# w3's first two row blocks transposed by VectorE, the others by TensorE with every eighth column

## The chip, the cores and the metric

The kernel runs on one core of a Trainium2 chip. The metric is the time of one execution on the device, in microseconds, as the median of several runs. TensorE does the matrix products, VectorE (DVE), ScalarE (ACT) and GpSimd (POOL) the elementwise work, and SyncE (SP) issues the loads and stores. Each engine takes its instructions in the order in which the program wrote them for it, and waits for others through semaphores.

## The reference

Three parts follow one another. A decay attention over 32 heads of 576 tokens with 64 columns gives x of 2304 tokens by 512. A gated product follows, and then a rational function between two products:

```
x    = attention(q, k, v, f)                 # 2304 x 512
c    = (x @ w1) * (x @ w2)                   # 2304 x 1024
z    = (c @ w3) @ w_out                      # w3 1024 x 1024, w_out 1024 x 512
h    = z @ w_in                              # 2304 x 2048
out  = (P(h) / Q(h)) @ w_out2                # P cubic, Q with abs(h) and h*h
```

The weights arrive as 64-bit floats. The kernel reads them as pairs of 32-bit integers and works out 32-bit floats from them.

## The kernel before

Every large product is made of three passes: an operand is split into a high half that TensorE's fast format holds and a low half that is the rest, and high x high, high x low and low x high are added in one PSUM bank. The high half is a ScalarE copy, the low half a VectorE or GpSimd subtraction.

The kernel never forms c @ w3. It first folds w3 @ w_out into one weight of 1024 x 512 (`w3oh`, `w3ol`), and then takes z = c @ (w3 @ w_out). The stages that matter here follow one another on TensorE:

- The last a/b products (`gen_ab`, lines 709 to 738). For each of 8 column blocks of w1 and w2 and each half of the last batch's 576 tokens there are 12 instructions for a = x @ w1 and 12 for b = x @ w2, 288 columns each: 16 pairs. ScalarE copies a out of PSUM, VectorE multiplies it with b, and SP stores the result to `c_dr`. Those steps wait in the list `pend` and are written out by `flush(keep)`, which leaves `keep` of them. The last batch uses two pairs of banks: `ps_f` 0 and 1, and the two halves of `ps_v`.
- The w3 stage (lines 1114 to 1139). For each row block i of w3 (128 rows) the block is transposed, split, and multiplied with w_out: 8 column blocks j times 3 passes of 512 columns into `ps_f[i % 2]`, and the result is split into `w3oh[:, i]` and `w3ol[:, i]` (lines 1130 and 1131, the fold). Block i + 1 is transposed by TensorE ahead of column block 2 of row i: 8 transposes of 128 x 128 into `ps_s` or `ps_x`, and right behind them ScalarE's and VectorE's halves (lines 1072 and 1073). Block 0 is transposed ahead of everything.
- The z products (lines 1187 to 1211): 9 blocks of 256 tokens, 4 column blocks each, 24 instructions of 256 columns per column block.

The decoder `dec_` (class `Decoder`, lines 164 to 246) turns weights into floats beside all this. Its jobs are pieces of 128 rows by 256 columns: 4 of w3's block 0, 16 of w_out, then w3's blocks 1 to 7, then 32 of w_in. One call of `step()` works on four neighbouring jobs, one operation of each: the low half of job k - 3 (VectorE twice out of three, GpSimd once), the high half of k - 2 (ScalarE), the sum of k - 1 (GpSimd, line 227), the first two operations of job k (VectorE, lines 231 and 234) and its conversion (ScalarE, line 237), and then SP's load of a job ahead into a ring of four. For w3 the two halves are left out. `run(n)` takes steps until job n is finished.

The order of the work around the change is written by hand. While the last a/b products are written, the loop at line 1083 writes 1600 ns of products (at 123 ns each), flushes, and takes one decoder step: 28 steps in all. In the w3 stage four steps follow per row, after column blocks 3, 4, 5 and 7, and one in the last row; in the z products one step follows each column block. `w3r` holds six decoded row blocks of w3, so that blocks 6 and 7 come into the places of 0 and 1. `load_c` reads c back for the z products, and `split_c` splits it on ScalarE and VectorE, two column blocks each at the end of rows 3 to 6.

Of the kernel before, what the change touches and what calls it, by code (L numbers as in the profile page):

```python
# [15 lines left out]
ALU = mybir.AluOpType  # L16
# [3 lines left out]
P = 128  # L20
# [9 lines left out]
PIECE2 = 256  # L30
# [129 lines left out]
def raw(ap):  # L160
    return ap.bitcast(F32)


class Decoder:
# [22 lines left out]
    def prefetch(self):  # L187
        while self.sent < min(self.upcoming() + self.ahead, len(self.jobs)):
            r = self.ring[self.sent % len(self.ring)]
            src = self.jobs[self.sent][0]  # L190
            dst = r.rearrange("p n t -> p (n t)")
            if len(src.shape) == 3:
                dst = dst.rearrange("p (k n) -> p k n", k=src.shape[1])
            self.nc.sync.dma_start(dst, src.bitcast(I32))
            self.sent += 1
# [130 lines left out]
def kernel(  # L326
# [16 lines left out]
    nc = tc.nc  # L343
    B, H, S, D = q.shape
    NT, DM = out.shape
    DF1 = w1.shape[1]
# [3 lines left out]
    NF1 = DF1 // P  # L350
# [27 lines left out]
    ident = const.tile([P, P], F32, name="ident")  # L378
# [12 lines left out]
    ps_v = psp.tile([P, 1024], F32, name="ps_v")  # L391
    ps_s, ps_x = ([psp.tile([P, 512], F32, name=f"ps_{nm}{i}") for i in range(2)] for nm in "sx")
# [3 lines left out]
    ps_f = []  # L396
# [271 lines left out]

    w12 = {}

    def split(h, l):
        nc.scalar.copy(h, raw(l))  # L672
        nc.vector.tensor_tensor(out=l, in0=raw(l), in1=raw(h), op=ALU.subtract)  # L673

    def open_w12():
        wp = right1.enter_context(pool("w12", "right"))
# [32 lines left out]
    def gen_ab(b, more=()):  # L709
        banks = [*ps_f, *more]  # L710
        X, L = xh[b % 2], xl[b % 2]
        n = 0
        FG = PIECE2 // P
        for g, hf, fi in itertools.product(range(NF1 // FG), range(2), range(FG)):
            ts_ = slice(HB * hf, HB * (hf + 1))
            fi += FG * g
            fs = slice(P * fi, P * (fi + 1))
            w12["dec"].run(4 * g + 3)
            outs = [t[:, 0:HB] for t in banks[n % (len(banks) // 2) * 2 :][:2]]
            for wi, nm in enumerate(("w1", "w2")):  # L720
                wh, wl = w12[nm]
                flush(len(banks) // 2)
                for kc in range(NKC):
                    mm(outs[wi], wh[:, kc, fs], X[:, kc, ts_], kc == 0, False)
                    yield 123
                    mm(outs[wi], wh[:, kc, fs], L[:, kc, ts_], False, False)
                    yield 123
                    mm(outs[wi], wl[:, kc, fs], X[:, kc, ts_], False, kc == NKC - 1)
                    yield 123
                if wi == 0:  # L730
                    pend.append(lambda a=a_sb[n % 2], o=outs[0]: nc.scalar.copy(a, o))

            def finish(c=c_sb[n % 3], a=a_sb[n % 2], fi=fi, hf=hf, o=outs[1]):
                nc.vector.tensor_tensor(out=c, in0=o, in1=a, op=ALU.mult)
                nc.sync.dma_start(c_dr[:, fi, S * b + HB * hf : S * b + HB * (hf + 1)], c)

            pend.append(finish)
            n += 1

    fillers = []  # L740
# [3 lines left out]
    def flush(keep=0):  # L744
        while len(pend) > keep:
            pend.pop(0)()
# [81 lines left out]
    for t in range(NCH * (NH + 1) + 2):  # L828
        n, c = divmod(t, NCH)
        p, x = n // 2, t % 2  # L830
# [198 lines left out]
    d3.close()  # L1029
    late.close()  # L1030
    att.close()
    fillers.append(gen_ab(B - 1, (ps_v[:, 0:512], ps_v[:, 512:1024])))

    r2 = ExitStack()
    zp = r2.enter_context(pool("zp", "left"))
    w3oh = zp.tile([P, NF1, DM], F32R, name="w3oh")
    w3ol = zp.tile([P, NF1, DM], F32R, name="w3ol")
    w3p = ExitStack()
    jobs = []
    dec_ = Decoder(nc, zp, "d2", PIECE2, 4, 4, jobs, "vvg")  # L1040
# [4 lines left out]
    NR3 = 6  # L1045
# [4 lines left out]
    wq = w3q.enter_context(pool("w3q", "left"))  # L1050
    w3r += [wq.tile([P, DF1], F32, name=f"w3r{i}") for i in range(NF1 - NR3, NR3)]

    def w3_jobs(i):
        for g in range(0, DF1, PIECE2):
            cs = slice(g, g + PIECE2)
            jobs.append((w3[P * i : P * (i + 1), cs], w3r[i % NR3][:, cs], None, None))

    def w_jobs(w, j, h, l):
        for g in range(0, w.shape[1], PIECE2):
            cs = slice(g, g + PIECE2)  # L1060
            jobs.append((w[P * j : P * (j + 1), cs], None, h[:, j, cs], l[:, j, cs]))

    def w3_transpose(i, g):
        ps = (ps_s, ps_x)[i % 2][g]
        for j in range(4):
            k = 4 * g + j
            nc.tensor.transpose(
                ps[:, P * j : P * (j + 1)], w3r[i % NR3][:, P * k : P * (k + 1)], ident
            )
        src = ps.rearrange("p (j t) -> p j t", t=P)  # L1070
        h, l = (t[i % 2][:, 4 * g : 4 * g + 4] for t in (w3h, w3l))
        nc.scalar.copy(h, src)
        nc.vector.tensor_tensor(out=l, in0=src, in1=raw(h), op=ALU.subtract)

    w3_jobs(0)
    for j in range(NF1):
        w_jobs(w_out, j, woh, wol)
    for i in range(1, NR3):
        w3_jobs(i)
    dec_.prefetch()  # L1080
    credit[0] = 0.0
    fill(3000.0)
    while fillers:
        fill(1600.0)
        flush(2)
        dec_.step()
    flush()
    right1.close()

# [8 lines left out]
    def load_c(i):  # L1098
        for g in range(0, NF1, 2):
            nc.sync.dma_start(  # L1100
                raw(cl[i % 2][:, g : g + 2]), c_dr[:, g : g + 2, T1 * i : T1 * (i + 1)]
            )

    def split_c(i, g):
        split(ch[i % 2][:, g : g + 2], cl[i % 2][:, g : g + 2])

    for i in range(NR3, NF1):
        w3_jobs(i)
    at_w3 = {i: 4 * i + (3 if i == 0 else 19) for i in range(NF1)}
    for kc in range(NKC):  # L1110
        w_jobs(w_in, kc, wih, wil)
    dec_.prefetch()
    load_c(0)
    for i in range(NF1):
        if i == 0:
            w3_transpose(0, 0)
            w3_transpose(0, 1)
        po = ps_f[i % 2]
        for j in range(NF1):
            if j == 2 and i + 1 < NF1:  # L1120
                dec_.run(at_w3[i + 1])
                w3_transpose(i + 1, 0)
                w3_transpose(i + 1, 1)
            elif j in ((3, 4, 5, 7) if i + 1 < NF1 else (3,)):
                dec_.step()
            h, l = w3h[i % 2][:, j], w3l[i % 2][:, j]
            mm(po, h, woh[:, j], j == 0, False)
            mm(po, h, wol[:, j], False, False)
            mm(po, l, woh[:, j], False, j == NF1 - 1)
        nc.scalar.copy(w3oh[:, i], po)  # L1130
        nc.vector.tensor_tensor(out=w3ol[:, i], in0=po, in1=raw(w3oh[:, i]), op=ALU.subtract)  # L1131
        if i + 1 == NR3 - 1:
            w3q.close()
            cp1 = ctx.enter_context(pool("cp1", "right"))
            ch.append(cp1.tile([P, NF1, T1], F32R, name="ch1"))
            cl.append(cp1.tile([P, NF1, T1], F32R, name="cl1"))
            load_c(1)
        if 3 <= i < 7:
            split_c(0, 2 * (i - 3))
    w3p.close()  # L1140

    wl_ = ctx.enter_context(pool("wl", "right"))
# [218 lines left out]
```

## Time and profile before

| what | us |
|---|---|
| median of 3 runs (lowest and highest) | 987.3 (986.68 to 989.33) |
| the profiled execution, its own time | 988.95 |
| its span, first to last instruction | 987.1 |
| TensorE busy | 972.3 |
| VectorE busy | 765.3 |
| ScalarE busy | 658.6 |
| GpSimd busy | 391.3 |

The span begins with the first instruction and ends with the last; the profiled execution's own time also holds what lies around it. Busy times of engines overlap. TensorE's matrix instructions overlap one another, so that the start of the next one, not the length of a row, tells what one costs. The last a/b products end at about 426 us of the span, the w3 stage runs to 477.6 us, the z products to 580.7 us. Granted clock of TensorE: 0.998 in the mean.

### The profile page before, as it was taken

The page shows a single profiled execution, that of the slowest core. Times are in us where ns is not written, and L with a number is a line of the kernel's source. Part 1 is how long each engine was busy: PE and PEld are TensorE (multiplying, and loading weights), DVE is VectorE, ACT ScalarE, POOL GpSimd, SP SyncE. Part 2 cuts the span into 40 slices and gives each one's busy share as a digit, 9 for nine tenths or more (in the row PEclk, how much of TensorE's full clock was granted, in tenths as well). Part 3 has the DMA queues.
Part 4 walks back from the last instruction along what each step waited for, and adds up shares of the span by engine and source line. Part 5 has one row for each costly group of instructions (what it writes and reads, how often), then busy time and mean ns, then how long its engine had stood idle before and what let it go on. Part 6 is the DMA issues. An engine that isn't in the chain of part 4 may idle for free.

```text
span 987.1 us, 18112 instructions
## 1 busy us (share of the span) xinstructions
PE 972.3 (98%) x5964; PEld 855.8 (87%) x5964; DVE 765.3 (78%) x1753; ACT 658.6 (67%) x1435; POOL 391.3 (40%) x468
## 2 busy tenths in 40 slices
PE   8999999999999999999999999999999999999997
PEld 6777999999999999988899998888888888888886
DVE  5777887878888766979866439999787888877786
ACT  5777676767777653444555448887676767676686
POOL 7477666644554443534433103232222222222222
PEclk9999999999999999999999999999999999999999
DMA  5777665677777515565467570011001100100010
GB/s 153 168 196 189 171 145 125 170 194 196 186 185 189 164 65 171 197 197 192 156 219 223 173 239 31 1 43 43 1 0 43 43 1 22 43 0 1 1 43 23
DMA packets 146470, 113.62 MB, mean 115 GB/s; under 512 B 86660, under 2 KB 113292, under 8 KB 146376
## 3 DMA queue, kind: packets, MB, share of 16 engines
q1 hardware_dynamic: 146376, 112.46, 40.2%
q8 instruction: 47, 0.77, 0.3%
q14 instruction: 47, 0.39, 0.1%
HBM read 70.61 MB, written 23.22 MB: 95 GB/s over the span
## 4 chain that ended last, share of the span: by engine, by line
PE 88%; DVE 4%; ACT 3%; issue 2%; DMA 1%; POOL 1%; SPq 1%; POOLq 0%; ACTq 0%; DVEq 0%
PE bank L366 47%; PE ps_f L366 20%; PE ps_v L366 7%; PE ps_s L366 6%; PE ps_x L595 5%; PE ps_w L366 1%; PE ps_v L443 1%; ACT rr L1272 1%; ACT rr L1273 1%; DVE pr L564 1%; DMA d_r<-in_moe_w_in_dram 1%; DVE pp L1285 1%; ACT gh L1253 0%; DVE rr L1281 0%; DVE qv L1278 0%
## 5 line engine op out<-in xcount | busy, mean ns | idle before, releaser
L1254 POOL TENSOR_TENSOR gl<-pp,gh 128x512 fp32r<-128x512 f32 (+1 forms) x80 | 101.4, 1268 | 330.7 <-ACT gh L1253 318.8
L590 POOL TENSOR_SCALAR pr<-pr,st 128x128 f32<-128x128 f32 (+4 forms) x160 | 95.2, 604 | 118.9 <-DVE st L585 62.5
L366 PE MATMUL bank<-ch,wil 128*128 128x512 f32 (+1 forms) x320 | 118.2, 370 | 0.0
L366 PE MATMUL bank<-cl,wih 128*128 128x512 f32 (+1 forms) x320 | 118.1, 369 | 0.0
L564 DVE CUSTOM_DVE_ANT_0 pr<-ps_s,mask 128x128 f32<-128x128 f32 (+4 forms) x160 | 82.6, 521 | 45.7 <-PE ps_s L366 37.2
L366 PE MATMUL bank<-ch,wih 128*128 128x512 f32 (+1 forms) x320 | 117.8, 368 | 0.0
L366 PE MATMUL bank<-wo2h,gh 128*128 128x512 f32 x288 | 114.2, 397 | 0.8 <-ACT gh L1253 0.8
L366 PE MATMUL bank<-wo2h,gl 128*128 128x512 f32 x288 | 114.0, 396 | 0.3
L366 PE MATMUL bank<-wo2l,gh 128*128 128x512 f32 x288 | 113.9, 396 | 0.0
L575 ACT ACTIVATE pr<-pr,st 128x128 f32<-128x128 f32 (+4 forms) x160 | 97.2, 608 | 17.1 <-DVE st L564 10.7
L1261 ACT ACTIVATE h<-bank 128x512 f32<-128x512 f32 (+1 forms) x80 | 44.3, 554 | 81.2 <-PE bank L366 81.1
L1268 DVE SCALAR_TENSOR_TENSOR qv<-h,pb_abs,qv 128x512 f32<-128x512 f32 (+1 forms) x80 | 55.6, 695 | 36.6 <-ACT qv L1262 36.6
L366 PE MATMUL bank<-ch,w3ol 128*128 128x256 f32 x288 | 81.0, 281 | 0.5 <-DVE w3ol L1131 0.5
L366 PE MATMUL bank<-cl,w3oh 128*128 128x256 f32 x288 | 81.0, 281 | 0.3 <-DVE cl L673 0.3
L366 PE MATMUL bank<-ch,w3oh 128*128 128x256 f32 x288 | 80.9, 281 | 0.0
L595 PE MATMUL ps_x<-ident,pr 128*128 128x128 f32 (+1 forms) x480 | 74.9, 267 | 2.3 <-DVE ptl L621 0.7
L366 PE MATMUL ps_s<-kh,qs 128*128 128x128 f32 (+2 forms) x192 | 74.0, 388 | 2.7 <-DVE st L564 1.2
L1278 DVE SCALAR_TENSOR_TENSOR qv<-qv,rr 128x512 f32<-128x512 f32 (+1 forms) x80 | 51.4, 643 | 25.7 <-ACT rr L1273 25.7
L366 PEld LDWEIGHTS bank<-cl,wih 128*128 128x128 f32 x320 | 60.2, 188 | 11.7
L366 PEld LDWEIGHTS bank<-ch,wih 128*128 128x128 f32 x320 | 60.2, 188 | 11.7
L673 DVE TENSOR_TENSOR cl<-cl,ch 128x512 fp32r<-128x512 f32 (+1 forms) x56 | 39.5, 724 | 38.7 <-ACT ch L672 38.5
L366 PEld LDWEIGHTS bank<-ch,wil 128*128 128x128 f32 x320 | 60.2, 188 | 10.3
(180 smaller groups left out, 2991.1 us busy)
## 6 DMA issues: line engine op xcount, KB each, us to landing
d_r<-in_moe_w_dram SPq DMA_DIRECT2D x64, 256.0 KB
d_r<-in_moe_w_out_dram SPq DMA_DIRECT2D x48, 256.0 KB
c_dr<-c_sb SPq DMA_DIRECT2D x64, 144.0 KB
cl<-c_dr SPq DMA_DIRECT2D x36, 256.0 KB
d_r<-in_moe_w_in_dram SPq DMA_DIRECT2D x32, 256.0 KB
kh<-kh SPq DMA_DIRECT2D x42, 144.0 KB
z_dr<-z_sb SPq DMA_DIRECT2D x36, 128.0 KB
out_dram<-o_sb SPq DMA_DIRECT2D x18, 256.0 KB
```

The lines of the kernel that those rows point to most:

```text
L366: nc.tensor.matmul(o, lhsT, rhs, start=start, stop=stop)
L443: nc.tensor.transpose(ps[:, P * c : P * (c + 1)], flat(t[:, c]), ident)
L564: nc.vector.tensor_tensor_reduce(out=pr[0:r, OFF[c] + a : OFF[c] + b], in0=ps_s[(t + part) % 2][0:r, 0 : b - a], in1=mask[0:r, 512 - Q0[c] ...
L575: nc.scalar.activation(x, x, AF.Exp, bias=st[0:r, 0, c : c + 1], scale=-1.0, accum_out=se[0:r, c, 0:1],)
L590: nc.gpsimd.tensor_scalar(x, x, st[0:r, 1, c : c + 1], 1.0, op0=ALU.mult, op1=ALU.mult)
L595: nc.tensor.transpose(ps_x[x][:, r * j : r * (j + 1)], pr[0:r, o + P * j : o + P * (j + 1)], ident[0:r, 0:r],)
L673: nc.vector.tensor_tensor(out=l, in0=raw(l), in1=raw(h), op=ALU.subtract)
L1254: nc.gpsimd.tensor_tensor(out=at(gl, j), in0=at(pp, j), in1=raw(at(gh, j)), op=ALU.subtract)
L1261: nc.scalar.activation(at(h2, i), h, AF.Square)
L1268: nc.vector.scalar_tensor_tensor(out=at(qv, i), in0=at(h2, i), scalar=pb_abs[:, 1:2], in1=at(qv, i), op0=ALU.mult, op1=ALU.add,)
L1272: nc.scalar.activation(at(rr, i), at(qv, i), AF.Ln, bias=ln_bias, scale=2.0**-62)
L1278: nc.vector.scalar_tensor_tensor(out=at(qv, i), in0=at(qv, i), scalar=QC, in1=at(rr, i), op0=ALU.add, op1=ALU.mult)
```

## The change

- `gen_ab` for the last batch has three pairs of banks: `ps_x` 0 and 1 come to `ps_f` and the halves of `ps_v`. `flush` still leaves two entries.
- Blocks 0 and 1 of w3 are loaded in another form: one piece is 32 rows by all 1024 columns, where partition 32 a + r holds row r and columns 256 a to 256 a + 255. VectorE transposes each half (128 x 512) in blocks of 32 x 32 into PSUM, reading every eighth column, so that partition p then holds columns 8 p + k of w3 for k from 0 to 7.
- Blocks 2 to 7 are transposed by TensorE as before, but each transpose takes every eighth column (k, k + 8, ...) in place of 128 neighbouring ones. w_out's rows are loaded in the same order (row 8 p + k), so that the sum runs over the same terms.
- The split of a transposed block is now a step of its own (`w3_split`). Block 0 is transposed and split within the loop over the last a/b products, from decoder step 20 on, one part ahead of each step. For block i + 1 the two halves of the transpose are written ahead of column blocks 2 and 3 of row i, and the two splits ahead of column blocks 4 and 5.
- The fold of row i is written ahead of column block 2 of row i + 1. Decoder steps follow ahead of column blocks 0, 1, 6 and 7 of rows 0 to 4, ahead of column block 0 in rows 5 and 6, and not at all in row 7.
- All of w3's jobs are in the list from the beginning; w_in's follow after the loop.
- `split` and `split_c` get an argument for the engine of the subtraction, which every call leaves at VectorE.

```diff
--- before.py
+++ after.py
@@ -189,7 +189,9 @@
             r = self.ring[self.sent % len(self.ring)]
             src = self.jobs[self.sent][0]
             dst = r.rearrange("p n t -> p (n t)")
-            if len(src.shape) == 3:
+            if len(src.shape) == 3 and src.shape[0] < P:
+                pass
+            elif len(src.shape) == 3:
                 dst = dst.rearrange("p (k n) -> p k n", k=src.shape[1])
             self.nc.sync.dma_start(dst, src.bitcast(I32))
             self.sent += 1
@@ -668,9 +670,9 @@
 
     w12 = {}
 
-    def split(h, l):
+    def split(h, l, on=nc.vector):
         nc.scalar.copy(h, raw(l))
-        nc.vector.tensor_tensor(out=l, in0=raw(l), in1=raw(h), op=ALU.subtract)
+        on.tensor_tensor(out=l, in0=raw(l), in1=raw(h), op=ALU.subtract)
 
     def open_w12():
         wp = right1.enter_context(pool("w12", "right"))
@@ -719,7 +721,7 @@
             outs = [t[:, 0:HB] for t in banks[n % (len(banks) // 2) * 2 :][:2]]
             for wi, nm in enumerate(("w1", "w2")):
                 wh, wl = w12[nm]
-                flush(len(banks) // 2)
+                flush(min(len(banks) // 2, 2))
                 for kc in range(NKC):
                     mm(outs[wi], wh[:, kc, fs], X[:, kc, ts_], kc == 0, False)
                     yield 123
@@ -1029,7 +1031,7 @@
     d3.close()
     late.close()
     att.close()
-    fillers.append(gen_ab(B - 1, (ps_v[:, 0:512], ps_v[:, 512:1024])))
+    fillers.append(gen_ab(B - 1, (ps_v[:, 0:512], ps_v[:, 512:1024], *ps_x)))
 
     r2 = ExitStack()
     zp = r2.enter_context(pool("zp", "left"))
@@ -1050,40 +1052,73 @@
     wq = w3q.enter_context(pool("w3q", "left"))
     w3r += [wq.tile([P, DF1], F32, name=f"w3r{i}") for i in range(NF1 - NR3, NR3)]
 
+    NA, NB, ND = P // 32, DF1 // PIECE2, 2
+
     def w3_jobs(i):
-        for g in range(0, DF1, PIECE2):
-            cs = slice(g, g + PIECE2)
-            jobs.append((w3[P * i : P * (i + 1), cs], w3r[i % NR3][:, cs], None, None))
+        for g in range(NB):
+            r0 = P * i + 32 * g
+            if i < ND:
+                rows = w3[r0 : r0 + 32].rearrange("i (a n) -> a i n", a=NA)
+            else:
+                rows = w3[P * i : P * (i + 1), PIECE2 * g : PIECE2 * (g + 1)]
+            jobs.append((rows, w3r[i % NR3][:, PIECE2 * g : PIECE2 * (g + 1)], None, None))
 
     def w_jobs(w, j, h, l):
         for g in range(0, w.shape[1], PIECE2):
             cs = slice(g, g + PIECE2)
             jobs.append((w[P * j : P * (j + 1), cs], None, h[:, j, cs], l[:, j, cs]))
 
+    def w_out_jobs(j):
+        rows = w_out.rearrange("(p k) n -> k p n", k=NF1)[j]
+        for g in range(0, DM, PIECE2):
+            cs = slice(g, g + PIECE2)
+            jobs.append((rows[:, cs], None, woh[:, j, cs], wol[:, j, cs]))
+
     def w3_transpose(i, g):
         ps = (ps_s, ps_x)[i % 2][g]
+        if i < ND:
+            src = w3r[i % NR3][:, 512 * g : 512 * (g + 1)]
+            nc.vector.transpose(
+                ps.rearrange("p (b k t) -> p b k t", b=2, t=32),
+                src.rearrange("p (b t k) -> p b k t", b=2, t=32),
+            )
+            return
+        cols = w3r[i % NR3].rearrange("p (t k) -> p k t", k=NF1)
         for j in range(4):
-            k = 4 * g + j
-            nc.tensor.transpose(
-                ps[:, P * j : P * (j + 1)], w3r[i % NR3][:, P * k : P * (k + 1)], ident
+            nc.tensor.transpose(ps[:, P * j : P * (j + 1)], cols[:, 4 * g + j], ident)
+
+    def w3_split(i, g):
+        ps = (ps_s, ps_x)[i % 2][g]
+        if i < ND:
+            src = ps.rearrange("p (b k t) -> p k b t", b=2, t=32)
+            h, l = (
+                t[i % 2][:, :, 64 * g : 64 * (g + 1)].rearrange("p k (b t) -> p k b t", t=32)
+                for t in (w3h, w3l)
             )
-        src = ps.rearrange("p (j t) -> p j t", t=P)
-        h, l = (t[i % 2][:, 4 * g : 4 * g + 4] for t in (w3h, w3l))
+        else:
+            src = ps.rearrange("p (j t) -> p j t", t=P)
+            h, l = (t[i % 2][:, 4 * g : 4 * g + 4] for t in (w3h, w3l))
         nc.scalar.copy(h, src)
         nc.vector.tensor_tensor(out=l, in0=src, in1=raw(h), op=ALU.subtract)
 
     w3_jobs(0)
     for j in range(NF1):
-        w_jobs(w_out, j, woh, wol)
-    for i in range(1, NR3):
+        w_out_jobs(j)
+    for i in range(1, NF1):
         w3_jobs(i)
+    at_w3 = {i: 4 * i + (3 if i == 0 else 19) for i in range(NF1)}
+    turned = 0
     dec_.prefetch()
     credit[0] = 0.0
     fill(3000.0)
     while fillers:
         fill(1600.0)
         flush(2)
-        dec_.step()
+        if turned < 4 and dec_.at >= 20:
+            (w3_transpose, w3_split)[turned // 2](0, turned % 2)
+            turned += 1
+        if dec_.at < 4 * NR3 + 16 or turned == 4:
+            dec_.step()
     flush()
     right1.close()
 
@@ -1101,34 +1136,36 @@
                 raw(cl[i % 2][:, g : g + 2]), c_dr[:, g : g + 2, T1 * i : T1 * (i + 1)]
             )
 
-    def split_c(i, g):
-        split(ch[i % 2][:, g : g + 2], cl[i % 2][:, g : g + 2])
-
-    for i in range(NR3, NF1):
-        w3_jobs(i)
-    at_w3 = {i: 4 * i + (3 if i == 0 else 19) for i in range(NF1)}
+    def split_c(i, g, on=nc.vector):
+        split(ch[i % 2][:, g : g + 2], cl[i % 2][:, g : g + 2], on)
+
     for kc in range(NKC):
         w_jobs(w_in, kc, wih, wil)
     dec_.prefetch()
     load_c(0)
+    def fold_out(i):
+        po = ps_f[i % 2]
+        nc.scalar.copy(w3oh[:, i], po)
+        nc.vector.tensor_tensor(out=w3ol[:, i], in0=po, in1=raw(w3oh[:, i]), op=ALU.subtract)
+
     for i in range(NF1):
-        if i == 0:
-            w3_transpose(0, 0)
-            w3_transpose(0, 1)
         po = ps_f[i % 2]
         for j in range(NF1):
-            if j == 2 and i + 1 < NF1:
-                dec_.run(at_w3[i + 1])
-                w3_transpose(i + 1, 0)
-                w3_transpose(i + 1, 1)
-            elif j in ((3, 4, 5, 7) if i + 1 < NF1 else (3,)):
-                dec_.step()
+            if j == 2 and i:
+                fold_out(i - 1)
+            if i + 1 < NF1:
+                if j == 2:
+                    dec_.run(at_w3[i + 1])
+                if j in (2, 3):
+                    w3_transpose(i + 1, j - 2)
+                if j in (4, 5):
+                    w3_split(i + 1, j - 4)
+                if j in (0, 1, 6, 7) and i < 5 or j == 0:
+                    dec_.step()
             h, l = w3h[i % 2][:, j], w3l[i % 2][:, j]
             mm(po, h, woh[:, j], j == 0, False)
             mm(po, h, wol[:, j], False, False)
             mm(po, l, woh[:, j], False, j == NF1 - 1)
-        nc.scalar.copy(w3oh[:, i], po)
-        nc.vector.tensor_tensor(out=w3ol[:, i], in0=po, in1=raw(w3oh[:, i]), op=ALU.subtract)
         if i + 1 == NR3 - 1:
             w3q.close()
             cp1 = ctx.enter_context(pool("cp1", "right"))
@@ -1137,6 +1174,7 @@
             load_c(1)
         if 3 <= i < 7:
             split_c(0, 2 * (i - 3))
+    fold_out(NF1 - 1)
     w3p.close()
 
     wl_ = ctx.enter_context(pool("wl", "right"))
```

## Rows read from the trace of the kernel before

**Rows 1.** busy time of each engine over the span, the page

```profile
PE 972.3 (98%) x5964; PEld 855.8 (87%) x5964; DVE 765.3 (78%) x1753; ACT 658.6 (67%) x1435; POOL 391.3 (40%) x468
```

**Rows 2.** busy time by stretch: stretch, length, each engine's busy time (instructions), clock, DMA

```profile
412.00:426.10 14.10, 14.10 (x108) 14.10 (x107) 11.74 (x24) 4.67 (x13) 7.03 (x10) 1.00 0.65 211
426.10:429.10 3.00, 2.76 (x16) 1.91 (x15) 1.75 (x3) 1.48 (x3) 0.00 (x0) 1.00 0.42 124
429.10:454.00 24.90, 24.90 (x127) 21.00 (x126) 21.67 (x42) 12.99 (x29) 10.48 (x14) 1.00 0.55 184
...
477.60:482.00 4.40, 3.61 (x27) 3.16 (x27) 4.33 (x9) 2.27 (x6) 2.43 (x4) 1.00 0.49 168
489.00:545.60 56.60, 56.60 (x483) 56.60 (x482) 36.90 (x69) 29.13 (x74) 20.45 (x26) 1.00 0.69 223
```

**Rows 3.** chain of waits, w3 stage: start, length, engine, tile, line, instructions

```profile
435.64 0.87 PE ps_s L1067 x8
436.52 5.46 PE ps_f L366 x24
```

**Rows 4.** TensorE in order of time, head of the w3 stage: start, length, instruction

```profile
426.10 1.04 PE L1067 MATMUL ps_s<-ident,w3r 128*128 128x128 f32 x8
...
429.13 1.03 PE L1067 MATMUL ps_x<-ident,w3r 128*128 128x128 f32 x8
```

**Rows 5.** TensorE in order of time, first z product

```profile
477.65 0.28 PE L366 MATMUL bank<-ch,w3oh 128*128 128x256 f32 x1
...
480.32 0.39 PE L366 MATMUL bank<-cl,w3oh 128*128 128x256 f32 x1 [0.27 <-DVE cl L673]
...
481.58 0.39 PE L366 MATMUL bank<-ch,w3ol 128*128 128x256 f32 x1 [0.52 <-DVE w3ol L1131]
```

**Rows 6.** TensorE in order of time, five transposes with 64 moving columns

```profile
158.96 0.52 PE L595 MATMUL ps_x<-ident,pr 64*128 64x64 f32 x5
```

**Rows 7.** instructions of line 595: ns shortest/median/longest, first and last start

```profile
L595 PE MATMUL ps_x<-ident,pr x480: 222/272/474, 18.7 to 368.9; 128*128 128x128 f32 x128, 64*128 64x64 f32 x32
```

**Rows 8.** instructions on tile ps_f, weight loads of the w3 products

```profile
L366 PEld LDWEIGHTS ps_f<-woh,w3h x64: 186/188/190, 427.4 to 476.7; 128*128 128x128 f32 x64
```

**Rows 9.** instructions of line 475, VectorE's transposes

```profile
L475 DVE STREAM_TRANSPOSE ps_v<-q_raw x9: 776/785/787, 129.4 to 318.7; 128x576 f32<-128x576 f32 x9
```

**Rows 10.** instructions on tile w3r, the decoder's two VectorE operations

```profile
L231 DVE TENSOR_SCALAR w3r<-d_r x32: 278/284/871, 379.8 to 461.0; 128x256 int32<-128x256 int32 x32
L234 DVE SCALAR_TENSOR_TENSOR w3r<-d_r,w3r x32: 424/859/1022, 380.2 to 461.3; 128x256 int32<-128x256 int32 x32
```

**Rows 11.** VectorE in order of time, end of the a/b products and w3 stage

```profile
420.33 0.46 DVE L734 TENSOR_TENSOR c_sb<-ps_v,a_sb 128x288 f32<-128x288 f32 x1 [0.47 <-ACT a_sb L731]
...
426.74 0.46 DVE L734 TENSOR_TENSOR c_sb<-ps_v,a_sb 128x288 f32<-128x288 f32 x1 [2.15 <-ACT a_sb L731]
...
433.41 0.28 DVE L231 TENSOR_SCALAR w3r<-d_r 128x256 int32<-128x256 int32 x1
...
434.62 0.29 DVE L231 TENSOR_SCALAR w3r<-d_r 128x256 int32<-128x256 int32 x1
...
444.27 0.28 DVE L231 TENSOR_SCALAR w3r<-d_r 128x256 int32<-128x256 int32 x1
...
449.40 1.29 DVE L1073 TENSOR_TENSOR w3l<-ps_s,w3h 128x512 fp32r<-128x512 f32 x2 [0.30 <-ACT w3h L1072]
...
450.61 0.28 DVE L231 TENSOR_SCALAR w3r<-d_r 128x256 int32<-128x256 int32 x1
...
457.78 0.28 DVE L231 TENSOR_SCALAR w3r<-d_r 128x256 int32<-128x256 int32 x1
...
480.84 0.68 DVE L1131 TENSOR_TENSOR w3ol<-ps_f,w3oh 128x512 fp32r<-128x512 f32 x1
```

**Rows 12.** ScalarE in order of time, w3 stage

```profile
434.68 0.44 ACT L237 ACTIVATE d_r<-d_r 128x256 int32<-128x256 uint32 x1 [2.86 <-DMA d_r<-in_moe_w_dram]
```

**Rows 13.** SP's queue in order of time, w3 stage

```profile
427.60 2.00 SPq L1100 DMA_DIRECT2D cl<-c_dr  x4
```

## The prediction

> **What bounds the kernel now.** I read the page's busy shares first, then the busy time by stretch, then the chain of waits, then each engine in order of time around the edit. The reader is to see that TensorE is busy for 98% of the span [rows 1], so that only its own time counts, and that in the edited stretch it is not merely busy but back to back: 14.10 of 14.10 us ahead of the w3 stage and 24.90 of 24.90 us inside it [rows 2]. The two places with a hole are the edges, 426.1 to 429.1 us (2.76 of 3.00) and 477.6 to 482 us (3.61 of 4.40). VectorE stands right behind: 21.67 of 24.90 us in the stage. So the question has two halves: what TensorE is spared, and whether VectorE, which takes work over, stays ahead.
>
> **What TensorE is spared.** Eight transposes take 0.87 us in the chain, so 0.109 us each, and 24 products of 512 columns 5.46 us, so 0.2275 us each [rows 3]. Blocks 0 and 1 of eight lose their 16 transposes: 16 x 0.109 = 1.75 us.
> The head of the stage: from the first transpose (426.10) to those of block 1 (429.13) pass 3.03 us [rows 4]. They hold 8 transposes (0.87) and 6 products (1.37); the other 0.8 us is waiting for ScalarE's and VectorE's halves of block 0, which after the change are made while the last a/b products still run. That wait goes.
> The tail: the first z product starts at 477.65; at 56.60/483 = 0.117 us each [rows 2] its 24th instruction would start at 480.34, and it starts at 481.58, held by a split of c and by the last low half of the folded weight [rows 5]. Those stand behind decoder steps on VectorE. After the change rows 5 to 7 of w3 carry two decoder steps in all (before: nine), and the last fold has only the one before it ahead: 1.2 us goes. Sum: 1.75 + 0.8 + 1.2 = 3.75 us.
>
> **What costs nothing, and its cover.** The third bank pair for the a/b products adds no instruction; TensorE already runs there without a hole. It is what hides VectorE's new delay: with two pairs a product that is taken 2 to 3 us late holds the next but one. The seven decoder steps that leave the stage are made among the z products; each is two or three VectorE, one or two ScalarE, one or two GpSimd instructions and one 256 KB load on SP's queue. VectorE is busy there for 36.90 of 56.60 us [rows 2], and seven steps at some 1.6 us are 11 us; the 33 steps needed fit into 36 places, so w_in is whole before its first product. If not, the next stage starts late by one step, 1.6 us. The other row order of w_out and of w3's first blocks moves the same 256 KB in the same 2 KB pieces; the ring of four hides it as before. The splits in a permuted order of 32-column runs I price as now.
>
> **What the 48 remaining transposes cost.** They now load their weights from every eighth float. No row shows such a load. From below: nothing, since the load is not what paces them. Five transposes with an identity of 64 columns, and the same 128 weight columns, stand for 0.52 us [rows 6]; with 0.27 for the last [rows 7] they are 0.062 apart, so a dense load takes at most that, and in the transposes here the 128 moving columns set the pace of 0.109. A gain is excluded for the same reason. From above: the loads of the products beside them stand 188 ns [rows 8]; nothing overlapped, that is 48 x (0.188 - 0.109) = 3.8 us. I take 0: even a load of twice the time stays at 0.124, near 0.109.
> The Trainium skill speaks against it: SBUF — State Buffer, Specifications (TRN2), wants two hits on each 16-byte line for full bandwidth, and every eighth float is 32 bytes on. TensorE: Matmul & The Clock Gate, LDWEIGHTS, gives columns/1.2, an estimate of 107 ns dense; the 62 ns spacing disagrees. Doubled to 213 ns by these two pages, the estimate is 48 x 0.104 = 5.0 us lost.
>
> **What VectorE gets.** Four transposes of 128x512. The nearest row is its transposes of 128x576 from dense rows, 785 ns [rows 9], by size 0.70 us. A gain is excluded, the elements are the same. From above, by the ratio of slowest to fastest of one form of instruction in this stage, 1022/424 [rows 10], 1.7 us. I take 0.70, the nearest row.
> A new wait comes with them: ScalarE's copy waits for VectorE's transpose, and behind it stand the decoder's conversions and the copies of a/b results, whose third bank pair allows them one product more, 24 x 14.10/108 = 3.1 us [rows 2].
> Two transposes and two splits (0.65 each, a pair is 1.29 [rows 11]) enter ahead of the last a/b results: 2.7 us. VectorE has 0.47 us idle there and is done at 426.74 - 2.15 = 424.59 [rows 11]; now at 424.59 + 2.7 - 0.47 = 426.8, then the last result (0.46), two steps (1.2 each, 434.62 - 433.41 [rows 11]), two transposes and the first split: 426.8 + 0.46 + 2.4 + 1.4 + 0.65 = 431.7. TensorE, which starts row 0 at 426.10, wants that low half with its 27th instruction, 426.10 + 26 x 0.2275 = 432.0. Just in time.
> For row 2 the split now stands behind four steps and a fold (before: behind the fold and waiting for the transpose, with 0.30 idle [rows 11]). Of the steps, the second needs a load that SP sends only after the four loads of c [rows 13]; ScalarE had it at 434.68 after 2.86 us of waiting [rows 12]. So 434.65 + 0.7 to 1.2 + 2.4 for two more + 0.62 + 0.62 = 439.0 to 439.5, wanted at 432.0 + 5.46 + 0.87 = 438.35: a wait of 0.6 to 1.1, I take 1.1 for what queues behind.
> From there a row costs VectorE 450.61 - 444.27 - 0.30 = 6.0 us [rows 11] against 6.33 of TensorE, and 457.78 - 450.61 = 7.2 where a split of c comes in. Two rows gain 0.3 each, the next loses 0.85 to 0.9: 0.3 to 0.6 more, I take 0.45. After that steps are few and no wait follows. Together 1.55 us.
> Forecast: -3.75 + 1.55 = -2.2 us. The profiled execution took 988.95 us (span 987.1 and 1.85 around it): 986.75 by its own count. The median of the runs is 1.65 lower, 987.3: so 985.1 us.
>
> **Rivals.**
> Full gain. VectorE keeps ahead: steps take 0.7 us whenever GpSimd is not adding beside them, and nothing in the trace forces the load of row 1 to be late by the amount I took. Against it: 21.67 of 24.90 us busy before the added work. No wait: 987.3 - 3.75 = 983.5.
> VectorE's transposes are slow on 32-byte steps. At 1.4 us the first low half comes at 431.7 + 4 x 0.7 = 434.5, a wait of 2.5 instead of 0; the second falls to 0.3, since everything has moved, the third stays 0.45. -3.75 + 3.25 = -0.5: 986.8; at 1.7 us, 1.2 more, 988.0. For: no row reads so wide a step. Against: the decoder's reads of every second word take 278 ns for 256 elements [rows 10], no more per element than a dense transpose, so steps as such cost nothing.
> The same line rule of the skill (SBUF — State Buffer) doubles these transposes to an estimate of 1.4 us.
> Slower: the strided weight load becomes TensorE's pace. Place: the 48 transposes of rows 2 to 7; at 188 ns each, 3.8 us. It decides from 0.109 + 2.2/48 = 0.155 us per transpose on, where the forecast's gain is gone: -2.2 + 3.8 = +1.6, 988.9. Against it: the dense load has room for 1.75 times its time under the moving columns.
> By the two pages' 213 ns this rival would give -2.2 + 5.0 = +2.8, an estimate of 990.1.
> That the change does not do what it says: the wait at 481.58 stays because the last fold cannot be made sooner than product and copy allow. Then 1.2 us of the gain is missing, 986.3; the fold's subtraction (0.68 [rows 11]) and a copy of like size fit into the 2.7 us before it is wanted, so I give this little and count it with the forecast.
>
> **How the numbers follow.** Forecast 0.42, full gain 0.28, slow VectorE transposes 0.15, slow weight load 0.15. A measurement of this kernel tells about 0.3% from no change, 3.0 us: faster means below 984.3, slower above 990.3. Faster: 0.25 of the full gain and 0.08 of the forecast's lower end, 0.33. Slower: 0.08 of the weight load (its upper part) and 0.04 for waits that add up beyond what I worked out, 0.12. Within: 0.55. The range reaches from the full gain less 0.7 us of scatter to the slower rival plus 0.7: 982.8 to 989.6.
>
> **What would show it.** In the trace after: 48 transposes on TensorE, 0.11 us apart (near 0.19 or more: the weight load); four VectorE transposes near 0.70 us (1.4: the line rule); no hole at the head of the stage, where the first w3 product follows the last a/b product at once; none near the 24th z instruction; small waits of TensorE for VectorE's low half near the start of w3's rows 2 and 5. The prediction is wrong if the w3 stage is not 1 us shorter, if a/b products wait for a bank, or if the z products wait for w_in's decoder.

## The result, and the profile after

The changed kernel takes 995.18 us in the median of 6 runs (994.77 to 998.14) against 987.4 us (985.89 to 989.59) for the kernel before: a ratio of 1.0078, 95% interval 1.0064 to 1.0092. It is slower by 7.8 us in the medians (7.7 by the ratio). The forecast was 985.1, the range 982.8 to 989.6: the time lies outside it, on the side that had 0.12.

The busy times of the changed kernel, from its page, answer to [rows 1]:

```profile
PE 970.4 (98%) x5948; PEld 852.7 (86%) x5948; DVE 768.2 (77%) x1757; ACT 657.8 (66%) x1435; POOL 392.0 (39%) x468
```

TensorE has 16 instructions fewer, as the change says, and is busy 1.9 us less, while the span is 995.0 us against 987.1. The loss is not added work: it is waiting and, as shown below, a lower clock. The windows of the changed kernel (columns as in [rows 2]) say where:

```profile
376.00:382.00 6.00, 6.00 (x46) 6.00 (x47) 1.09 (x3) 0.85 (x2) 0.53 (x1) 1.00 0.27 96
412.00:426.10 14.10, 12.50 (x91) 11.81 (x89) 11.22 (x23) 4.50 (x13) 5.28 (x7) 1.00 0.40 132
426.10:430.00 3.90, 3.46 (x24) 3.23 (x24) 2.68 (x7) 1.92 (x6) 1.14 (x2) 1.00 0.62 204
430.00:434.30 4.30, 0.00 (x0) 0.00 (x0) 4.23 (x8) 1.87 (x5) 2.54 (x4) 0.75 0.53 162
434.30:439.00 4.70, 4.67 (x11) 3.72 (x12) 4.35 (x9) 1.01 (x3) 2.23 (x3) 0.50 0.86 262
439.00:454.00 15.00, 15.00 (x75) 12.61 (x75) 12.89 (x25) 7.64 (x17) 6.16 (x8) 1.00 0.66 208
489.00:545.60 56.60, 56.60 (x482) 56.51 (x480) 37.86 (x70) 30.58 (x78) 19.30 (x24) 1.00 0.61 195
```

The stretch ahead of the w3 stage, full before (14.10 of 14.10), now has 12.50, and for 4.3 us TensorE does nothing at all. Behind that its granted clock is 0.50: 11 instructions in 4.7 us, 0.43 us apart where 0.23 is the rule. TensorE's instructions in order of time, those that waited in these stretches, and two at the lower clock:

```profile
398.28 0.40 PE L368 MATMUL ps_v<-xh,w1h 128*128 128x288 f32 x1 [0.86 <-DVE c_sb L736]
...
424.23 0.40 PE L368 MATMUL ps_x<-xh,w2h 128*128 128x288 f32 x1 [1.46 <-DVE c_sb L736]
...
426.50 0.40 PE L368 MATMUL ps_f<-xh,w1h 128*128 128x288 f32 x1 [0.41 <-ACT a_sb L733]
...
434.32 0.80 PE L368 MATMUL ps_f<-woh,w3h 128*128 128x512 f32 x1 [4.37 <-ACT a_sb L733]
...
435.77 0.63 PE L368 MATMUL ps_f<-woh,w3h 128*128 128x512 f32 x1
436.20 0.63 PE L368 MATMUL ps_f<-wol,w3h 128*128 128x512 f32 x1
...
567.76 0.38 PE L368 MATMUL bank<-cl,w3oh 128*128 128x256 f32 x1 [0.69 <-DVE cl L675]
568.90 0.39 PE L368 MATMUL bank<-cl,w3oh 128*128 128x256 f32 x1 [0.18 <-DVE cl L675]
```

The a/b products now wait for a bank, and the first w3 product waits 4.37 us for the bank that the last copy of a empties. That copy is ScalarE's last instruction in this stretch, and ScalarE in order of time shows what stood ahead of it:

```profile
428.78 0.44 ACT L239 ACTIVATE d_r<-d_r 128x256 int32<-128x256 uint32 x1 [1.85 <-DMA d_r<-in_moe_w_dram]
...
430.44 0.44 ACT L239 ACTIVATE d_r<-d_r 128x256 int32<-128x256 uint32 x1 [0.58 <-DMA d_r<-in_moe_w_dram]
430.78 0.38 ACT L733 COPY a_sb<-ps_x 128x288 f32<-128x288 f32 x1
431.46 0.43 ACT L239 ACTIVATE d_r<-d_r 128x256 int32<-128x256 uint32 x1 [0.30 <-DMA d_r<-in_moe_w_dram]
433.55 0.44 ACT L239 ACTIVATE d_r<-d_r 128x256 int32<-128x256 uint32 x1 [1.65 <-DMA d_r<-in_moe_w_dram]
433.89 0.38 ACT L733 COPY a_sb<-ps_f 128x288 f32<-128x288 f32 x1
```

The decoder's conversion (L239) waits for a load, and the copy stands behind it. The chain of waits names one load of the same tensor for the 10 us before:

```profile
418.22 10.47 DMA d_r<-in_moe_w_dram
```

The idle time that ended with such a load, from the view by tile (us, times), is in the kernel before

```profile
  DMA d_r<-in_moe_w_dram: 18.2, 17
```

and in the changed one

```profile
  DMA d_r<-in_moe_w_dram: 55.4, 39
```

The account closes on three milestones. TensorE's first instruction of the w3 stage comes at 434.32 instead of 426.10 [rows 4], 8.2 us late. The stage takes 51.54 us against 51.55, of which some 10 products at 0.43 us instead of 0.23 are about 2.0, an estimate, so it is about 2.0 shorter apart from the clock. The z products take 102.77 against 103.08. 8.2 - 0.0 - 0.3 = 7.9, the whole of 995.0 - 987.1.

### The profile page after: what moved, and what is told of

Read it like the earlier page. It is cut to its first block, busy times and chain, and to the rows that moved or that the text cites. A ratio compares the mean times of both kernels' runs of the same rounds, so it can differ in the third digit from the quotient of the medians.

```text
span 995.0 us, 18069 instructions
## 1 busy us (share of the span) xinstructions
PE 970.4 (98%) x5948; PEld 852.7 (86%) x5948; DVE 768.2 (77%) x1757; ACT 657.8 (66%) x1435; POOL 392.0 (39%) x468
## 4 chain that ended last, share of the span: by engine, by line
PE 84%; DVE 5%; DMA 4%; ACT 2%; issue 2%; POOL 2%; SPq 0%; POOLq 0%; ACTq 0%; DVEq 0%
PE bank L368 46%; PE ps_f L368 20%; PE ps_s L368 6%; PE ps_x L597 5%; PE ps_v L368 4%; DMA d_r<-in_moe_w_dram 2%; PE ps_w L368 1%; DMA z_dr<-z_sb 1%; DVE d_f L233 1%; ACT rr L1311 1%; ACT rr L1310 1%; DVE pr L566 1%; DVE wol L220 1%; DVE pp L1323 0%; POOL pr L592 0%
```

## The experiments

Two theories at the outset. Loads: blocks 0 and 1 arrive too slowly in their new form, and everything queued behind the decoder is late. Queues: the new places of copies, steps and VectorE's transposes hold the banks, and the slow load is only what they wait for by chance. Each ratio below is to executions of the kernel before that were taken beside the run (medians 988.09 to 988.52 us).

**Only the loads, in the kernel before.** The eight pieces of blocks 0 and 1 get the new form, nothing else changes. It moves the rows of those blocks to other places, so the product is another one of the same size. The decoder's branch for this form, as in the change, is left out here:

```diff
-            jobs.append((w3[P * i : P * (i + 1), cs], w3r[i % NR3][:, cs], None, None))
+            rows = w3[P * i : P * (i + 1), cs]
+            if i < 2:
+                r0 = P * i + 32 * (g // PIECE2)
+                rows = w3[r0 : r0 + 32].rearrange("i (a n) -> a i n", a=4)
+            jobs.append((rows, w3r[i % NR3][:, cs], None, None))
```

> The kernel before, with nothing of the change but the form of the loads of w3's blocks 0 and 1 (outermost dimension 4). The blocks then hold w3's numbers in another order, so the product is not the reference's. Theory A: 3 to 8 us slower than before (990 to 995), with the decoder's 21st step some 6 us later and a wait of TensorE at the end of the a/b products. Theory B: 986 to 989, as before.

Measured: 996.72 us, ratio 1.0087 (1.0073 to 1.0101). The loads alone cost 8.6 us, all of the loss and a little more. The window of block 0's loads, columns as in [rows 2], for the kernel before and then with the new form of load:

```profile
376.00:382.00 6.00, 5.77 (x44) 5.57 (x43) 2.10 (x5) 1.54 (x4) 1.13 (x2) 1.00 0.67 211
...
376.00:382.00 6.00, 6.00 (x48) 6.00 (x47) 1.09 (x3) 0.84 (x2) 0.46 (x1) 1.00 0.25 85
```

The same transfers in 40 slices (busy tenths of 16 DMA engines), first for the kernel before:

```profile
DMA  0089704499814898998899779979997310060018
GB/s 0 31 323 369 246 16 96 150 164 191 123 41 123 219 355 300 341 382 341 314 369 341 301 287 341 314 300 369 355 355 273 137 55 27 27 109 0 0 54 315
```

and then with the new form of load:

```profile
DMA  0015001123222222222222222222222228222222
GB/s 0 0 14 27 0 14 41 68 82 82 82 82 96 109 82 109 96 109 96 109 96 109 96 109 82 109 96 109 109 82 109 109 96 218 82 96 109 109 96 96
```

The plain loads keep 7 to 9 tenths busy at some 340 GB/s. The new ones lie flat at 2 tenths and some 100 GB/s from the tenth slice on, but for one slice.

This kernel loses its time on another path than the changed one:

```profile
387.48 0.61 PE L368 MATMUL ps_v<-xh,w1h 128*128 128x288 f32 x1 [3.46 <-DVE c_sb L736]
```

With two pairs of banks TensorE waits 3.46 us already at 387.48 us, for VectorE's product behind the decoder's work on block 0, and its granted clock is 0.50 from there to 392 us; behind block 1's loads it waits only 1.55 and 0.99 us. The changed kernel, which has three pairs, waits 0.86 us before block 1's loads come (at 398.28) and loses most behind them. The loads are the cause in both; that 8.6 and 7.8 lie so near each other is in part chance.

**The changed kernel with each piece loaded in four parts** of 32 partitions, one DMA each.

```diff
             if len(src.shape) == 3 and src.shape[0] < P:
-                pass
+                for a in range(src.shape[0]):
+                    self.nc.sync.dma_start(dst[32 * a : 32 * (a + 1)], src[a].bitcast(I32))
+                self.sent += 1
+                continue
```

> The changed kernel, but each load of w3's blocks 0 and 1 is issued as four loads of 32 partitions by 256 columns, in place of one load whose outermost dimension is 4. Same bytes, same places. Theory A (a load with an outermost dimension of 4 runs on 4 of the 16 DMA engines, the decoder falls behind and ScalarE's queue with it): the DMA share during these loads rises from about 0.25 to over 0.6, the hole of 4.4 us ahead of the w3 stage and TensorE's half clock behind it go, and the time falls from 995 to 984 to 988 us. Theory B (VectorE's transposes of 1.17 us and their place in its queue are what delays the a/b results): the time stays within 2 us of 995.

Measured: 987.49 us, ratio 0.999 (0.998 to 1.0001). The loss is gone. The window of the first loads and the end of the a/b products, columns as above:

```profile
376.00:382.00 6.00, 6.00 (x48) 6.00 (x47) 1.81 (x5) 1.68 (x4) 1.47 (x2) 1.00 0.46 140
412.00:426.10 14.10, 13.44 (x102) 13.20 (x100) 12.53 (x27) 6.04 (x16) 6.62 (x9) 1.00 0.63 194
```

The share is 0.46 where plain loads had 0.67 (211 GB/s): better than 0.27, short of the 0.6 that was expected. SP's queue spends 8.47 us on the 16 parts of block 0, where it spent 1.82 us on four plain loads; whether that is what holds the share down, no run here shows. Instructions on the decoder's ring still wait 44.7 us for these loads, and TensorE 1.41 us at the head of the stage and 0.87 for block 1's high half.

**Fewer things queued ahead of the last copies.** The last three decoder steps are written behind the flush, with the slow loads kept.

```diff
-        if dec_.at < 4 * NR3 + 16 or turned == 4:
+        if dec_.at < 25:
             dec_.step()
     flush()
+    dec_.step()
+    dec_.step()
+    dec_.step()
```

> The changed kernel, but the last three decoder steps of the a/b loop are written behind the flush of the last results, so that ScalarE's last copies of a stand ahead of three conversions that wait for loads. If the hole of 4.4 us is ScalarE's queue (a copy that is ready stands behind a conversion that waits for a load), the hole shrinks by 2 to 4 us and the time is 990 to 993. If the copy is late for itself or for VectorE's sake, the time stays at 994 to 996.

Measured: 996.55 us, ratio 1.0089 (1.0076 to 1.0101), and the expectation missed. TensorE in order of time:

```profile
431.96 0.50 PE L368 MATMUL ps_f<-woh,w3h 128*128 128x512 f32 x1 [1.75 <-ACT a_sb L733]
...
441.50 0.50 PE L368 MATMUL ps_f<-woh,w3h 128*128 128x512 f32 x1 [2.19 <-ACT w3h L1101]
```

The first wait falls from 4.37 to 1.75 us, and a new one of 2.19 stands at row 1. Behind each the granted clock falls again (0.61 from 432 to 436 us, 0.85 from 445 to 450). So the first w3 product comes 2.4 us earlier than in the changed kernel (431.96 against 434.32), and the first z product 1.4 us later (487.30 against 485.86). The order decides where the late load is felt, the load decides that it is. The queue theory fails as the cause of the loss.

**No block on VectorE.** `ND = 0`: all loads plain, all 64 transposes on TensorE, everything else of the change kept.

> The changed kernel with no block transposed by VectorE: all eight by TensorE from every eighth column, all loads in the usual form. Measures the rest of the change (early block 0, later splits and folds, fewer steps, third bank pair). Theory A and B alike: 985.5 to 988, since both bad causes are gone; the head of the w3 stage has no hole, 64 transposes stay on TensorE. If instead it stays above 992, the cause is in the rest of the change.

Measured: 987.92 us, ratio 0.9998 (0.9988 to 1.0007). There is no wait at the head or in the w3 stage. So the third bank pair, the later folds and splits, the moved steps and the reading of every eighth column cost nothing together, and gain nothing that can be told: the 0.8 us at the head is gone, but 1.03 us of waits stand among the z products.

**The same with four decoder steps in rows 5 and 6 as well,** to have w_in's floats earlier.

```diff
-                if j in (0, 1, 6, 7) and i < 5 or j == 0:
+                if j in (0, 1, 6, 7):
                     dec_.step()
```

> The changed kernel with no block transposed by VectorE, and with four decoder steps in rows 5 and 6 too. There the w3 stage has no wait, and about 1.2 us are lost among the z products near 536 and 558 us, where c's split is late. If that comes from the decoder steps that the change moves there, six steps fewer end it: 986.3 to 987.2 against 987.9. If it comes from the stores and loads of the z stage themselves, 987.5 to 988.5.

Measured: 991.86 us, ratio 1.0028 (1.0014 to 1.0042), a miss. Its executions lie between 987.72 and 992.6 us, and the profile is of one of 992.13. There the z products wait 0.60 us instead of 1.03, but the last row waits for a fold that stands behind those steps:

```profile
474.77 0.47 PE L368 MATMUL ps_f<-woh,w3h 128*128 128x512 f32 x1 [3.09 <-DVE w3ol L1149]
```

A fold that is written two column blocks later needs the steps out of its way.

**Two pairs of banks instead of three,** on the four-part version: `ps_x` is left out of `gen_ab`'s banks.

> The changed kernel with the four-piece loads, but with two pairs of banks for the last batch's a/b products as before the change. The prediction held that the third pair hides the delay of VectorE's transposes in that stage. If so, TensorE waits for VectorE's a/b results (0.5 to 3 us in all) and the time rises from 987.5 to 988 to 990.5. If VectorE's delay is small enough by itself, 987 to 988.

Measured: 989.56 us, ratio 1.0017 (1.0008 to 1.0027), 2.1 us above the four-part version by the medians, 2.7 by the ratios. The a/b products wait for a bank again, and the row behind them for a fold:

```profile
398.68 0.40 PE L371 MATMUL ps_v<-xh,w1h 128*128 128x288 f32 x1 [0.73 <-DVE c_sb L739]
...
441.60 0.47 PE L371 MATMUL ps_f<-woh,w3h 128*128 128x512 f32 x1 [1.00 <-DVE w3ol L1152]
```

**Dense reads in both transposes,** on the four-part version. This mixes the rows of the folded weight; the instructions are the same in number and size.

```diff
-                src.rearrange("p (b t k) -> p b k t", b=2, t=32),
+                src.rearrange("p (b k t) -> p b k t", b=2, t=32),
...
-        cols = w3r[i % NR3].rearrange("p (t k) -> p k t", k=NF1)
+        cols = w3r[i % NR3].rearrange("p (k t) -> p k t", k=NF1)
```

> The changed kernel with the four-piece loads, but TensorE's transposes load 128 neighbouring columns and VectorE's transposes read 32 neighbouring ones, in place of every eighth (the folded weight then mixes rows that do not belong together). Measures the stride alone. For VectorE: 0.70 us in place of 1.13 to 1.19 if the step of 32 bytes is what it pays for, 1.1 or more if it is the 128x512 form itself. For TensorE: transposes 0.109 us apart either way, with weight loads of 140 in place of 190 ns. The time 0.5 to 1.5 us under 987.5 if VectorE's 1.9 us less shorten the wait at the start of row 1, and 987 to 988 if loads set that wait.

Measured: 988.67 us, ratio 1.0002 (0.9992 to 1.0011): no time gained. The groups by line (ns shortest/median/longest), strided in the changed kernel:

```profile
L1081 DVE STREAM_TRANSPOSE ps_s<-w3r x2: 1165/1176/1187, 417.6 to 419.6; 128x512 f32<-128x512 f32 x2
...
L1088 PEld LDWEIGHTS ps_s<-ident,w3r x24: 186/190/193, 443.2 to 470.4; 128*128 128x128 f32 x24
L1088 PE MATMUL ps_s<-ident,w3r x24: 272/273/276, 443.4 to 470.5; 128*128 128x128 f32 x24
```

and dense in this one:

```profile
L1084 DVE STREAM_TRANSPOSE ps_s<-w3r x2: 711/716/720, 415.0 to 416.2; 128x512 f32<-128x512 f32 x2
...
L1091 PEld LDWEIGHTS ps_s<-ident,w3r x24: 137/140/143, 435.1 to 463.9; 128*128 128x128 f32 x24
L1091 PE MATMUL ps_s<-ident,w3r x24: 270/272/273, 435.4 to 464.0; 128*128 128x128 f32 x24
```

The stride costs VectorE 0.45 us per transpose and a weight load 50 ns. From the first of four transposes to the product behind them pass 0.36 us either way (443.43 to 443.79 strided, 435.35 to 435.71 dense), so TensorE loses nothing to it.

**The queues in a better order,** on the four-part version: all copies of a drained in the last round of the loop, and a row's decoder steps behind its splits.

```diff
-        flush(2)
+        flush(2 if fillers else 0)
...
-                if j in (0, 1, 6, 7) and i < 5 or j == 0:
+                if j in (6, 7) and i < 5:
+                    dec_.step()
+                    dec_.step()
+                elif j == 7:
                     dec_.step()
```

> The changed kernel with the four-piece loads, and two places of its order changed: the last copies of a are written ahead of the last decoder step of the a/b loop, and in the w3 stage all decoder steps of a row stand behind that row's splits (two ahead of column block 6, two ahead of block 7; one in rows 5 and 6). Theory: with the loads on all engines, what is left of TensorE's waiting (1.4 us at the head, 0.9 us at the start of row 1, each with a slower first instruction behind it) is order in ScalarE's and VectorE's queues, a ready copy behind a conversion that waits for its load, and a split behind two decoder steps. Then both waits go and the time falls 1.5 to 3 us under the four-piece kernel, to 984.5 to 986. Rival: the loads themselves are late, and the wait only moves to a later row; then it stays within 1 us of the four-piece kernel (987.5).

Measured: 986.37 us, ratio 0.9985 (0.9976 to 0.9994). The time is above the expected range, and the interval overlaps that of the four-part version. Both waits of that version are gone; in their place stand 0.66 us for a fold's low half and 1.50 among the z products, where the four-part version had none.

**That order with one block on VectorE** (`ND = 1`) **and with none** (`ND = 0`).

> The better order of the queues (last copies of a drained in the loop, two decoder steps after a row's splits) with four-piece loads and VectorE for block 0 alone; block 1 is loaded plainly and transposed by TensorE. If the waits left in the two-block version (0.66 us for the fold's low half, 1.5 us at the z products' decoder) come from block 1's slower loads and VectorE's long transposes, they go, and 0.87 us of transposes comes back: 985.4 to 986.4, ratio to before about 0.998. Rival: those waits come from where the steps and folds stand; then they stay, and only the 0.87 us is added: about 987.2, ratio 0.9995.

> The same order with no block on VectorE and all loads plain: 1.75 us of transposes come back to TensorE. If loads and VectorE's transposes made the remaining 2.2 us of waits: 985.9 to 986.9, ratio about 0.999. Rival (the waits belong to the order): 988, ratio 1.0005.

Measured: 986.25 us, ratio 0.9976 (0.9966 to 0.9985) with one block, and 986.95 us, 0.9984 (0.9974 to 0.9993) with none. The windows of the version with one block:

```profile
412.00:426.10 14.10, 14.10 (x107) 14.04 (x106) 13.75 (x29) 6.46 (x17) 7.21 (x10) 1.00 0.60 193
426.10:480.00 53.90, 53.90 (x283) 46.08 (x281) 38.95 (x76) 24.34 (x54) 19.62 (x25) 1.00 0.52 170
```

TensorE is without a hole from the a/b products through the head of the z products; the stage takes 425.66 to 475.87, 50.21 us instead of 51.55. So the 0.66 us did come from block 1's loads and transposes, as expected; the z products' 1.5 us did not: they are there with one block (1.50) and with none (2.37). This version beats both kernels, by 0.24% over the kernel before. The intervals of the three versions in this order overlap, so how many blocks VectorE should take is not told by their times. In their profiles the first z product comes at 476.40 us with none, 475.87 with one and 476.34 with two (477.65 in the kernel before): of the 0.87 us of transposes per block the first gives back 0.5 and the second nothing, by one execution each.

## Why the prediction was wrong

**The step that failed** is one sentence: the other row order "moves the same 256 KB in the same 2 KB pieces; the ring of four hides it as before", priced at nothing, with no bound and no rival. Bytes and pieces are the same, but the form of the load is not: its outermost dimension has 4 entries where the plain one has 128. The share lies at 0.25 of 16 DMA engines while such loads run, and 256 KB at some 100 GB/s take 2.6 us where 340 GB/s take 0.8. In the run that changed only the loads, ScalarE's four conversions of block 0 start at 380.45, 383.14, 386.19 and 389.00 us, 2.7 to 3.1 apart. The ring of four doesn't hide it, because the loop takes a step about every 1.6 us. Measured price: 8.6 us, from the run with nothing else changed, and 7.7 by the medians (8.7 by the ratios) from the run that took it away. The four-part loads bring the same rows to the same places, so the places are not the cause. No run changed the outermost size alone, to 8 for instance; that this size is the reason rests on the share of 0.25, which is 4 of 16.

The Trainium skill states such a rule, in DMA: Bandwidth & Descriptors, Why a DMA increments its semaphore by 16 and not by 1: one DMA is spread over the largest number of engines up to 16 that divides the slowest dimension of both sides, which for 4 entries is 4. The trace agrees: 4 of 16 is 0.25, and the row lies flat at 2 tenths.

The load didn't reach TensorE directly. It held the decoder's conversions; these held copies of a on ScalarE; these held banks; and the idle time cost once more through the clock, about 2.0 us at a granted 0.50, the lower of its two levels (1.2 of 2.4 GHz), after 4.4 us without an instruction. The prediction had named what stands behind VectorE's new wait on ScalarE, and counted one late load, row 2's, but none that its form makes slow.

Two of the signs that the prediction set against itself came: the w3 stage is not shorter (51.54 us against 51.55), and a/b products wait for a bank (0.86, 1.46 and 0.41 us). With the loads in four parts the change gives 0.6 us by the medians (987.49 against 988.09, an interval that holds no change), not the 2.2 forecast.

**The other steps, against the runs.**

- 16 transposes, 1.75 us: not told apart from the rest. The instructions are gone, and the w3 stage, less the clock's 2.0, is about 2.0 shorter than before, but that holds the wait at its head too. The 1.9 us by which TensorE's busy time fell are no measure: in the first 100 us, ahead of the change, it is already 2.3 us less (90.04 against 92.35). In the better order one block gave 0.5 of its 0.87 us, two gave nothing more.
- The head, 0.8 us: it goes where the copies aren't late (no wait in the versions with the better order).
- The z products' head, 1.2 us: the waits at 480.32 and 481.58 [rows 5] are gone in the changed kernel. But later blocks wait 1.21 us for a split of c, so the z products are only 0.3 us shorter.
- The third pair as cover: right, 2.1 us without it by the medians.
- Strided weight load, 0 taken and 3.8 as the bound: 0. The load takes 190 ns instead of 140 and stays covered. The slower rival that rested on it is refuted. But the step to that 0 misread [rows 7]: 272 ns is the median of two forms together, and the transposes with 64 columns take 231 ns in the mean, so they are (0.52 - 0.231)/4 = 0.072 us apart and not 0.062. Twice that is 0.145, above 0.109; the 0 is right, and this step doesn't show it.
- VectorE's transposes, 0.70 us taken: 1.12 to 1.19. The nearest row was dense, and dense ones do take 0.72; the rival with 1.4 us was nearer. It cost no time that can be measured here (0.9992 to 1.0011 against 0.998 to 1.0001).
- VectorE's waits, 1.55 us: in the four-part version 2.28 us stand in the stage, 1.41 of them for a copy of a and 0.87 for a high half on ScalarE; none is for the split on VectorE as worked out, and the better order removes them.
- "The seven decoder steps cost nothing": in part. The version that put six of them back lost 2.8 us by its ratio, to a fold in the w3 stage, which tells nothing of their price among the z products; these wait between 0 and 2.4 us by version, without a pattern that these runs resolve.

What stays open is that last item. In the changed kernel the chain runs from a late store of z (5.00 us in transfer) through ScalarE's copy of z and a split of c to the product. The four-part version, with the same steps, has no such wait in its profile. One execution of each doesn't tell its cause, and no run varied it alone.

## What to carry to other kernels

When a load's form changes, read the size of its outermost dimension on both sides before its bytes: with 4 there, a load had a share of 0.25 of the DMA engines, and a row of the transfers that lies flat at 2 tenths shows it at once. Where a decoder's loads arrive just in time, a slow load is paid for by whoever stands behind the decoder in an engine's queue; moving that engine's work moves the wait and doesn't shorten it. The gain of a moved wait counts only after the next stage has been looked at: here 1.2 us came back as 1.21.

## What the runs showed of the hardware

- Loads of 256 KB whose outermost dimension is 4 ran at some 100 GB/s; the stretch had a share of 0.25 and 85 GB/s. Cut into four loads of 32 partitions each, it had 0.46 and 140 GB/s, and in the plain form 0.67 and 211 GB/s.
- TensorE's granted clock was 0.50 behind 4.4 us without an instruction (changed kernel) and behind 3.5 us (loads alone); it also fell behind waits of 1.75 and 2.19 us in one run, and stayed at 1.00 behind 1.41 and 0.87 us in another.
- VectorE's transpose of 128x512 f32 took 0.69 to 0.72 us from dense rows and 1.12 to 1.19 us from every eighth float. By SBUF — State Buffer, Specifications (TRN2), of the Trainium skill, a step of 32 bytes loses bandwidth; the trace agrees with a factor of 1.6, less than the 2 that the prediction drew from it.
- TensorE's weight load from every eighth float took 190 ns against 140, and its transposes did not come further apart.
